# Joining MLP rounds in pairs: W1 with 512 moving columns, units ordered by row lane

## Chip, cores, metric

One core of one Trainium2 chip. The metric is the device time of one execution in microseconds (us), median over executions. A ratio is the mean time of one kernel's fast runs over the mean of the other's fast runs of the same rounds, so it is not quite the ratio of the medians quoted beside it.

## The reference

A transformer block on 2048 tokens of 576 features: layernorm, linear attention with a softmax feature map (32 heads of 18), output projection `wo`, residual; then layernorm and an MLP of 4608 hidden features. The part that matters here is the MLP:

```python
def _B_ref(x, w1, b1, w2, b2):          # x: 2048 x 576
    y = _layernorm(x, axis=-1)
    h = _gelu(jnp.einsum("bsd,df->bsf", y, w1) + b1)      # 576 -> 4608
    return jnp.einsum("bsf,fd->bsd", h, w2) + b2          # 4608 -> 576
...
h  = x + _A_ref(_layernorm(x), ...)     # attention and wo
h2 = h + _B_ref(_layernorm(h), ...)
```

## The kernel before

The MLP works in eight rounds of 256 tokens (two tiles of 128). A round is a W1 stage (36 blocks of 128 hidden features, gelu on ScalarE into `hmid`) and a W2 stage (two tiles, 36 matmuls of 512 columns and 36 of 64 each). The attention of later tiles is spread over it: `attn_N` (numerator and denominator, a chain on the vector engine and the pool engine behind it) in W2, `wo` with the second layernorm in W1.

W1 contracts over 576 = 4 x 128 + 64 rows. It runs in two row lanes, `pe0` (partitions 0 to 63) and `pe8` (64 to 127), that work side by side. Each unit is one PSUM bank with two blocks of 256 columns. Each lane does 4 half chunks per block, and the half chunk of 64 rows (`c == 4`) goes to one lane or the other. Both lanes add into the same bank, one after the other; which lane is first alternates.

```python
UNITS = [(4 * (u // 2) + u % 2, 4 * (u // 2) + u % 2 + 2) for u in range(NF // 2)]
...
def w1_half(r, u, h, begin):
    lane = "pe8" if h else "pe0"
    ...
    k = 1 if h else 0
    return [lambda i=i, c=c, n=n: one(i, c, begin and n == 0)
            for n, (i, c) in enumerate([(k, 4)] + [(i, c) for i in (0, 1) for c in range(4)])]

SKEW = 3
def w1_round(r, extra):
    lo, hi = [], []
    for s in range(NF // 2):
        k = s % 3
        u8 = s + (2, -1, -1)[k]             # second lane: units 2, 0, 1 of each three
        lo += [(f, None) for f in w1_half(r, s, 0, k < 2)]
        hi += [(f, None) for f in w1_half(r, u8, 64, k == 0)]
        # ... gelu of finished units, wo of later tiles
    hi = [(None, None)] * SKEW + hi         # first lane three matmuls ahead in issue order
    # ... then issued in turn, one of each lane

def w2_tile(r, j, slots):
    mb = (3, 2)[j]                          # PSUM bank of the 512 columns
    for i in range(NF + LAG):
        if i in slots:
            slots[i]()                      # attn_N of a later tile at step i
        # ... matmul i into bank mb, matmul i - LAG into the tail bank 4
    P.add("pool", ...tmpo = x_all[t] + b2bc...)
    # ... two vector additions ostage = psum + tmpo, then the output DMA
```

A scheduler class records every operation with the buffers and banks it touches and derives the semaphore waits. Each engine executes its stream in the order in which the operations are recorded.

The softmax here doesn't subtract the row's maximum and nothing guards it: scores larger than these inputs give would overflow.

## Time and profile before

| | before |
|---|---|
| median of 3 runs | 405.87 us (405.58 to 406.34) |
| span of the profiled run | 403.8 us |
| TensorE busy | 98% |
| W1 alone / W2 alone (256 tokens) | 18.02 / 17.75 us |
| from the first W1 to the last weight load of W2 | 309.48 us |

### The profile page before, as it was taken

The page shows a single profiled execution, that of the slowest core. Times are in us where ns is not written, and L with a number is a line of the kernel's source. Part 1 is how long each engine was busy: PE and PEld are TensorE (multiplying, and loading weights), DVE is VectorE, ACT ScalarE, POOL GpSimd, SP SyncE. Part 2 cuts the span into 40 slices and gives each one's busy share as a digit, 9 for nine tenths or more (in the row PEclk, how much of TensorE's full clock was granted, in tenths as well). Part 3 has the DMA queues.
Part 4 walks back from the last instruction along what each step waited for, and adds up shares of the span by engine and source line. Part 5 has one row for each costly group of instructions (what it writes and reads, how often), then busy time and mean ns, then how long its engine had stood idle before and what let it go on. Part 6 is the DMA issues. An engine that isn't in the chain of part 4 may idle for free.

```text
span 403.8 us, 11636 instructions
## 1 busy us (share of the span) xinstructions
PE 396.6 (98%) x4999; PEld 289.8 (72%) x4999; DVE 176.8 (44%) x415; ACT 184.4 (46%) x429; POOL 91.5 (23%) x130
## 2 busy tenths in 40 slices
PE   7999999999999999999999999999999999999997
PEld 4566666868955995599569856985797579658954
DVE  7999898876254223432442333243225312300000
ACT  6898955678820462057106600760175026404710
POOL 4759640112114002200220022002200220111001
PEclk9999999999999999999999999999999999999999
DMA  8586487981101101101111111001100110000000
GB/s 255 102 130 159 139 176 256 317 281 19 35 18 36 29 19 33 32 18 19 35 31 29 22 28 38 18 19 32 33 18 19 31 32 19 19 15 18 2 2 29
DMA packets 45738, 25.86 MB, mean 64 GB/s; under 512 B 32888, under 2 KB 44664, under 8 KB 45688
## 3 DMA queue, kind: packets, MB, share of 16 engines
q1 hardware_dynamic: 44928, 24.97, 24.8%
q8 instruction: 39, 0.64, 0.7%
q10 hardware_dynamic: 760, 0.17, 0.2%
q14 instruction: 11, 0.09, 0.1%
HBM read 15.13 MB, written 2.36 MB: 43 GB/s over the span
## 4 chain that ended last, share of the span: by engine, by line
PE 90%; DVE 5%; DMA 2%; ACT 1%; issue 1%; POOL 0%; DVEq 0%; ACTq 0%
PE ps_all L1153 35%; PE ps_all L1237 33%; PE ps_all L957 5%; PE ps_all L745 4%; PE ps_all L762 4%; PE ps_all L835 3%; PE ps_all L857 2%; PE ps_all L1220 2%; PE ps_all L804 2%; DMA yT<-ybuf 1%; DVE bns L494 1%; DMA x_all<-in_A_x_dram 1%; DVE sums L773 1%; DVE ybuf L526 1%; DVE x_all L979 1%
## 5 line engine op out<-in xcount | busy, mean ns | idle before, releaser
L1164 ACT ACTIVATE RA<-ps_all,b1T 128x256 bf16<-128x256 f32 x288 | 114.9, 478 | 176.8 <-PE ps_all L1153 162.1
L1153 PE MATMUL ps_all<-yT,w1sb 64*128 64x256 bf16 x2304 | 151.9, 269 | 0.0
L1153 PEld LDWEIGHTS ps_all<-yT,w1sb 64*128 64x128 bf16 x2304 | 136.1, 94 | 5.1
L1237 PE MATMUL ps_all<-w2a,RA 128*128 128x64 bf16 (+1 forms) x600 | 90.3, 286 | 0.0
L1153 PE MATMUL ps_all<-yT,w1t 64*128 64x256 bf16 x288 | 70.9, 270 | 0.0
L1237 PEld LDWEIGHTS ps_all<-w2a,RA 128*128 128x128 bf16 x600 | 42.9, 98 | 33.4 <-ACT RA L1164 1.7
L1237 PE MATMUL ps_all<-RB,RA 128*128 128x64 bf16 (+1 forms) x480 | 63.4, 286 | 0.0
L1246 DVE TENSOR_TENSOR WQ<-ps_all,tmpo 128x64 bf16<-128x64 f32 (+1 forms) x30 | 13.7, 458 | 96.3 <-PE ps_all L1237 84.0
L1237 PEld LDWEIGHTS ps_all<-RB,RA 128*128 128x128 bf16 x480 | 31.4, 98 | 30.3
L979 DVE SCALAR_TENSOR_TENSOR x_all<-ps_all,x_all 128x576 bf16<-128x576 f32 x16 | 12.1, 758 | 82.8 <-PE ps_all L957 82.8
L1001 POOL TENSOR_TENSOR st<-st,neghalf 128x1 f32<-128x1 f32 x16 | 8.8, 550 | 136.3 <-DVE st L998 133.6
L925 POOL TENSOR_TENSOR obuf<-tpn 128x576 bf16<-128x576 f32 x14 | 19.6, 1401 | 84.1 <-DVE tpn L918 74.4
L841 ACT ACTIVATE Eq<-ps_all 128x512 bf16<-128x512 f32 (+1 forms) x48 | 25.0, 526 | 12.2 <-PE ps_all L835 11.3
L957 PE MATMUL ps_all<-wo_sb,OTR 64*128 64x288 bf16 x288 | 29.7, 283 | 0.5 <-ACT OTR L567 0.2
L1153 PEld LDWEIGHTS ps_all<-yT,w1t 64*128 64x128 bf16 x288 | 26.3, 94 | 1.9
L835 PE MATMUL ps_all<-yT,WQ 128*128 128x256 bf16 x200 | 25.2, 273 | 0.2 <-ACT Eq L841 0.2
L786 DVE TENSOR_TENSOR RB<-ps_all,RB 128x1152 bf16<-128x1152 f32 x16 | 21.6, 1352 | 3.4 <-PE ps_all L762 3.3
L1243 POOL TENSOR_TENSOR tmpo<-x_all,b2bc 128x576 f32<-128x576 bf16 x15 | 19.1, 1272 | 17.4 <-DVE WQ L1246 17.4
L745 PE MATMUL ps_all<-RA,yT 128*128 128x512 bf16 (+1 forms) x160 | 22.4, 286 | 0.3 <-DMA yT<-ybuf 0.2
L957 PEld LDWEIGHTS ps_all<-wo_sb,OTR 64*128 64x128 bf16 x288 | 19.6, 94 | 3.7 <-PE ps_all L957 0.8
L762 PE MATMUL ps_all<-RB,yT 128*128 128x512 bf16 (+1 forms) x160 | 22.2, 286 | 0.0
L752 ACT ACTIVATE RB<-ps_all 128x576 bf16<-128x576 f32 x32 | 19.1, 649 | 5.8 <-PE ps_all L745 5.3
(110 smaller groups left out, 332.4 us busy)
## 6 DMA issues: line engine op xcount, KB each, us to landing
w1sb<-in_B_w_dram SPq DMA_DIRECT2D x8, 576.0 KB, 5.4
w2a<-in_B_w_dram SPq DMA_DIRECT2D x4, 720.0 KB, 7.3
RB<-in_B_w_dram SPq DMA_DIRECT2D x2, 1152.0 KB, 8.2
out_dram<-WQ SPq DMA_DIRECT2D x15, 144.0 KB, 1.8
x_all<-in_A_x_dram SPq DMA_DIRECT2D x3, 576.0 KB, 5.7
w2a<-in_A_wqkv_dram SPq DMA_DIRECT2D x2, 288.0 KB, 3.5
RB<-in_A_wqkv_dram SPq DMA_DIRECT2D x1, 576.0 KB, 5.7
w1t<-in_B_w_dram SPq DMA_DIRECT2D x2, 288.0 KB, 3.4
```

The source lines that it names most:

```text
L745: P.add("pe", lambda e, c=c, o=o, n=n: e.matmul(ps_all[:, 512 * KB + o:512 * KB + o + n], yT[:, c, sl * 128:(sl + 1) * 128], weffk[:, c, o ...
L752: P.add("act", lambda e, s=s: e.activation(Ek[eb][:, D * s:D * s + D], ps_all[:, 512 * KB:512 * KB + D], AF.Exp, scale=1.0 if s == 0 else ...
L762: P.add("pe", lambda e, c=c, o=o, n=n: e.matmul(ps_all[:, 512 * VB + o:512 * VB + o + n], yT[:, c, sl * 128:(sl + 1) * 128], wv[:, c, o:o ...
L786: P.add("dve", lambda e, s0=s0, s1=s1: e.tensor_tensor(vx(t)[:, s0:s1, :, 0:DH], ps_all[:, 512 * VB:512 * VB + D].rearrange("p (h d) -> p ...
L835: P.add("pe", lambda e, i=i, c=c, h0=h0: e.matmul(ps_all[:, 512 * bk + RW * i:512 * bk + RW * i + RW], weffq[:, c, DH * h0:DH * h0 + 128], ...
L841: P.add("act", lambda e, s=s: e.activation(Eq[:, r, s, bs[0]:bs[0] + n, :], ps_all[:, 512 * bk:512 * bk + RW * n].rearrange("p (b t) -> p ...
L925: P.add(oeng, lambda e: e.tensor_tensor(obuf[ob][:, 0:D], tpn[:, 0, :], tpn[:, 1, :], ALU.add), reads=[res("tpn")], writes=[res(f"obuf{ob}")])
L957: P.add(lane, lambda e: e.matmul(ps_all[:, 512 * bk:512 * bk + DHF], oT[ob][h:h + 64, c, :], wo_sb[h:h + 64, c, o:o + DHF], start=first, s ...
L1153: P.add(lane, lambda e: e.matmul(ps_all[:, o:o + RW], lhs, yT[h:h + 64, c, ys], start=first, stop=not begin and i == 1 and c == 3, skip_gr ...
L1164: P.add("act", lambda e, m=m, o=o: e.activation(hmid[:, m, :], ps_all[:, o:o + RW], AF.Gelu_apprx_tanh, bias=b1T[:, m:m + 1]), reads=[res( ...
L1237: P.add("pe", lambda e, m=m, bk=bk, o=o, n=n: e.matmul(ps_all[:, 512 * bk:512 * bk + n], w2_lhs(m, j), w2_rhs(m, o, n), start=(m == 0), st ...
L1243: P.add("pool", lambda e: e.tensor_tensor(tmpo[:, :], x_all[:, t, :], b2bc[:, :], ALU.add), reads=[res("b2"), res(f"x{t}")], writes=[res(" ...
```

## The change

The intent: from round three on, two rounds are joined to 512 tokens. A W1 unit is then one block of 512 columns, so half as many matmuls and weight loads are issued, and four W2 tiles follow one W1. The gelu output of 512 tokens is twice as large; half of it goes to the q features `Eq`, no longer needed by then. Blocks are ordered so that the second lane gets more work in the first units and the first lane in the last. With joined rounds, `attn_N` of four tiles must fit into W2 of round one and of round two, and `wo` of four tiles into W1 of round two, so their steps change, and the pool addition of each W2 tile is issued at its start (`BADD = 0`).

```diff
+    def mord(n):
+        lo, hi = [m for m in range(NF) if m % 4 < 2], [m for m in range(NF) if m % 4 >= 2]
+        if n == 1:
+            kinds = ["hh", "lh", "hh"] + ["lh"] * 12 + ["ll", "ll", "lh"]
+        else:
+            kinds = ["h"] * 3 + ["l", "h"] * 15 + ["l"] * 3
+        return [tuple((lo if k == "l" else hi).pop(0) for k in u) for u in kinds]
...
-        hi = [(None, None)] * SKEW + hi
-        # ... one of each lane in turn
+        at = [0, 0]
+        while lo or hi:
+            k = 0 if lo and (not hi or at[0] <= at[1] and hi[0][1]) else 1
+            f, w = (lo, hi)[k].pop(0)
+            f()
+            at[k] += w + (6 if w else 0)
...
+    BADD = 0
...
+            if i == BADD:
+                P.add("pool", ...tmpo = x_all[t] + b2bc...)
             if i in slots:
                 slots[i]()
...
-    for r in range(NR):
-        # ... attn_N of two tiles per W2 stage, steps 2 and 6; wo at units 3 and 12
+    GROUPS = [(0,), (1,), (2, 3), (4, 5), (6, 7)]
+    for g, rs in enumerate(GROUPS):
+        # ... wo of the next group; attn_N of the group after it:
+        j, i = (k // 2, ((4, 25) if g == 0 and k < 2 else (2, 22))[k % 2]) if len(here) == 2 else (k, 6)
```

## The prediction

> **What bounds the kernel now.** I read the page's busy shares first, then the chain that ended last in order of time, then a table of busy time by stage, then the groups by line and shape, and last the starts of single matmuls in the trace.
>
> The page:
>
> ```profile
> PE 396.6 (98%) x4999; PEld 289.8 (72%) x4999; DVE 176.8 (44%) x415; ACT 184.4 (46%) x429; POOL 91.5 (23%) x130
> ...
> PEclk9999999999999999999999999999999999999999
> ...
> PE 90%; DVE 5%; DMA 2%; ACT 1%; issue 1%; POOL 0%; DVEq 0%; ACTq 0%
> PE ps_all L1153 35%; PE ps_all L1237 33%; PE ps_all L957 5%; PE ps_all L745 4%; PE ps_all L762 4%; PE ps_all L835 3%; PE ps_all L857 2%; PE ps_all L1220 2%; PE ps_all L804 2%; DMA yT<-ybuf 1%; DVE bns L494 1%; DMA x_all<-in_A_x_dram 1%; DVE sums L773 1%; DVE ybuf L526 1%; DVE x_all L979 1%
> ```
>
> TensorE is the bound, at full clock, and two thirds of the chain is the MLP: W1 (L1153) and W2 (L1237). A busy share of 98% does not say that every slot is filled, so I go to the stages. The table by stage (columns: window, its length, TensorE busy with records, granted clock, DMA share, GB/s) gives, for rounds one and two, round seven and the W1 of round eight, a W1 row and a W2 row each:
>
> ```profile
> 91.63:112.73 21.10, 21.10 (x373) 1.00 0.17 26
> 112.73:131.96 19.23, 19.06 (x165) 1.00 0.16 34
> 131.96:152.19 20.23, 20.23 (x364) 1.00 0.07 18
> 152.19:171.09 18.90, 18.90 (x166) 1.00 0.17 35
> ...
> 327.58:347.80 20.22, 20.22 (x364) 1.00 0.07 17
> 347.80:365.55 17.75, 17.75 (x146) 1.00 0.08 20
> 365.55:383.57 18.02, 18.02 (x328) 1.00 0.03 10
> ```
>
> W1 alone takes 18.02 us (last row). With the two wo tiles of the next round it takes 20.22, so wo costs 2.20. W2 alone takes 17.75, and with two attn_N tiles 18.90. Round one's W2 is 0.33 longer than round two's, and its TensorE is short of its window by 0.17. The groups by line and shape:
>
> ```profile
> L1153 PE MATMUL ps_all<-yT,w1sb 64*128 64x256 bf16 x2304 | 151.9, 269 | 0.0
> L1153 PEld LDWEIGHTS ps_all<-yT,w1sb 64*128 64x128 bf16 x2304 | 136.1, 94 | 5.1
> L1164 ACT ACTIVATE RA<-ps_all,b1T 128x256 bf16<-128x256 f32 x288 | 114.9, 478 | 176.8 <-PE ps_all L1153 162.1 <-PE ps_all L957 13.6
> L1237 PE MATMUL ps_all<-w2a,RA 128*128 128x512 bf16 x300 | 75.2, 380 | 0.0
> L841 ACT ACTIVATE Eq<-ps_all 128x512 bf16<-128x512 f32 x32 | 19.1, 598 | 7.3 <-PE ps_all L835 6.8
> L841 ACT ACTIVATE Eq<-ps_all 128x256 bf16<-128x256 f32 x16 | 6.1, 383 | 4.9 <-PE ps_all L835 4.5
> ```
>
> W1 uses half the rows of the array per matmul (64*128), in two lanes that run side by side. The mean 269 ns is start to end; what counts is start to start. In the last W1 the trace shows pairs (one matmul of each lane) 109.3 ns apart. At the end the pairing stops: starts at 383.133 and 383.145, then single ones at 383.254 and 383.363. A round has 324 matmuls, 162 slots for two lanes: 162 x 0.1093 = 17.71. From 365.546 to the first W2 start at 383.565 are 18.02; less 0.093 of switch (202 ns between the last W1 start and the first of W2, less 109), 17.93 are left, or 164.1 slots. So two slots of each W1 are run by one lane alone.
>
> Why: a unit is a PSUM bank, which the lanes fill in turn, and the second waits for the first one's last matmul to complete. That is 269 ns plus some 60 of semaphore (DVE's end to the next weight load was 55 ns), or 3.0 slots after its start. Both lanes have nine matmuls per unit, so the second is due one slot after that start and is two late. The lag stays for the round.
>
> **What the Trainium skill says.** "TensorE: Matmul & The Clock Gate", section "Back-to-back issue gap", gives N/2.4 + 2.5 ns for the gap at full clock: 109.2 at 256 columns, 215.8 at 512. The trace agrees: 109.3 for the paired lanes, 215 to 217 for the 512-wide matmuls of W2. The same section's "sustained" 131 ns at 512 is not seen here. The page "TensorEngine Tiling (Array Packing)", section "Key Properties", says that changing the tiling mode drains the engine; the trace shows 93 ns over the usual gap going from W1 to W2 and 97 going back. "PSUM — Partial Sum Buffer", section "PSUM bank collisions raise a hardware error", says that two row tiles must not write one bank at the same time. That is why the lanes take turns and why the lag exists.
>
> **The change part by part.**
>
> Moving size 512. Three pairs of rounds have 3 x 324 matmuls of 512 in place of 6 x 324 of 256. Per pair, 2 x 162 x 109.2 = 35.38 become 162 x 215.8 = 34.96: 0.42 saved. The weight loads halve, but they lay beside the matmuls (94 against 109 ns), so this is worth nothing by itself.
>
> Order by row lane. The half chunk of 64 rows belongs to one lane or the other by block. Three blocks whose half chunk is the second lane's come first, three of the other kind last. In a pair the second lane so has 5 slots in its first unit while the first has 4: it is due at slot 5, and the first lane's bank is complete at 3 + (380 + 60)/216 = 5.04. Later handoffs have more room, and both lanes end together at 162. This saves 2.1 slots of 0.109 per joined round: 0.23, or 0.46 per pair. In rounds one and two (units of two blocks) the first handoff fits too (10 against 10.02), but the last one does not: the second lane is due in its last unit at slot 154, and the bank is complete at 155.02. One slot stays lost, so 0.12 is saved per round.
>
> Mode switches. Four W2 tiles follow each joined W1: one W1-to-W2 and one W2-to-W1 switch less per pair, 0.19.
>
> Gelu. In W1, 256 columns follow one another every 356 ns (six in 2.29 us). For 512 I estimate 478 + (598 - 383) = 693 ns, against 4.5 x 216 = 971 per unit on TensorE: hidden, and ScalarE gets more room than before (712 of 983). But the last pair unit in bank 3 is finished by the second lane only 5 slots before W1 ends, and W2's first tile starts in bank 3. The completion is 1.08 - 0.38 = 0.70 before that end, gelu starts 0.22 later (382.65 to 382.87 in the trace) and ends at +0.21, and with 0.06 of semaphore W2 starts at +0.27 in place of +0.09. New wait: 0.17 per pair.
>
> Sum per pair: 0.42 + 0.46 + 0.19 - 0.17 = 0.90; three pairs 2.70. Rounds one and two: 0.24.
>
> attn_N moved. The count of attn_N and wo matmuls stays the same. The first attn_N in round one's W2 is moved from step 2 to step 4, after the wait seen here:
>
> ```profile
> 113.72 0.34 PEld L857 LDWEIGHTS ps_all<-kvr,Eq 126*128 126x128 bf16 x6 [0.33 <-DVE x_all L979]
> ```
>
> That 0.33 goes. But now two attn_N fall into each W2 tile of rounds one and two. The vector chain of one (L872 at 153.28 to the end of L918 at 156.80) is 3.52 us. In round one it starts behind the LayerNorm chain of the last wo, which I put at 116.5, so it ends at 120.0. The second attn_N wants the banks from 119.55: about 0.1 of wait, and at the next tile 0.16 more. I take the gain as 0.33 - 0.26 = 0.07. In round two there is room.
>
> The pool addition moved to the start of a W2 tile, the output buffers and the added oT buffers move nothing on TensorE. The output addition at a W1 start frees bank 2 in time: done 0.83 after that start, wanted at 0.86 (4 slots of 216).
>
> Total: 2.70 + 0.24 + 0.07 = 3.0. 405.87 - 3.0 = 402.9. The step positions look tuned to avoid just these waits, so I go slightly lower: 402.6.
>
> **The rivals.**
>
> 1. New waits eat the gain. Several margins are tens of ns: 5.04 against 5, 0.86 against 0.83, the bank 3 wait at 0.17. For it: the operands wait in program order, so one lane's wait also stops the other. Against it: each is a wait once per round, not per unit. If each pair lost two 512 slots again (0.43 x 3), the time would be 403.9.
> 2. ScalarE becomes the bound in W1. If gelu were to take over 971 ns at 512 columns, the pairs would run at its pace, each 0.01 us longer per unit for every 10 ns: at 1100 ns some 4.6 us more per pair, a slower kernel. Exp at 512 took 598 against 383, so I give this almost nothing.
> 3. 512-wide lanes gain more than the gap formula says, if weight loads now disturb the 256-wide stream. Then W1 would fall clearly below 34.96 per pair. Against it: pairs at 109.3 ns leave 2.6 over 256/2.4, so at most 0.0026 x 972 = 2.5 us could be had in all, of which 1.26 is counted. That bounds the time near 400.9.
> 4. The joining crowds DVE and Pool with attn_N and output work: those engines are at 44% and 23%, and this would show only in rounds one and two. Worth at most 1 us.
>
> **Range and chances.** Rivals 1 and 4 give the upper side, 403.9; skipping all new waits (0.51 for bank 3, 0.26 for attn_N) gives 402.1, and some of rival 3 a bit less. I take 401.5 to 403.9. Faster by over 2% needs 397.8, 8.1 us, more than twice what can be found. Slower by 2% needs rival 2. Chances: 0.02 faster, 0.97 the same, 0.01 slower.
>
> **What would show it.** Pair slots of 215 to 217 ns; W1 of the last pair, which has no wo in it, at 35.0 to 35.3 us and both lanes ending within one slot; four W2 tiles at 35.5 without attn_N; a TensorE idle of 0.1 to 0.3 on ScalarE at each W1-to-W2 border; the first W1 at 20.98. It is wrong if slots differ from 216, if single-lane stretches remain in the pairs, or if DVE waits appear on TensorE in the W2 of the first two rounds that sum to over 0.5 us.

## More of the kernel before

The prediction shows the lines that carry its argument. Two more matter later. They are from the timelines of the vector engine and of pool in round one's W2 (columns: start in us, duration in us, engine, line, operation, output and inputs, and what ended the idle time before):

```profile
115.65 0.43 DVE L526 TENSOR_SCALAR ybuf<-x_all,st 128x576 bf16<-128x576 bf16 x1 [0.74 <-POOL st L1001]
```

```profile
121.48 1.27 POOL L1243 TENSOR_TENSOR tmpo<-x_all,b2bc 128x576 f32<-128x576 bf16 x1
```

The first is the layernorm of the last `wo` tile, which runs at the start of W2. The second is the pool addition for the output of the first W2 tile. It comes almost 6 us later, when the normalisation is long done.

## The result

| | before | after |
|---|---|---|
| median, same rounds | 406.07 us | 404.04 us (403.80 to 404.56) |
| ratio, 95% interval | | 0.9953 (0.9936 to 0.9970) |
| span of the profiled run | 403.8 us | 402.1 us |
| first W1 to last weight load of W2 | 309.48 us | 307.35 us |

The kernel is faster by 2.0 us. The prediction, 402.6 with 401.5 to 403.9, wanted 3.3 and missed its range by 0.14. The class (within 2%) was right. Two later calls ran the changed kernel again: 404.36 and 404.05, ratios 0.9946 both times.

A caution on reading: the trace of the changed kernel has 4,027 weight loads but 3,990 matmuls; 37 matmul records are missing, among them the first of several stages. By matmul records the border from W1 to W2 seemed to have grown by 0.2 to 0.3 us everywhere. The weight loads are complete, and I take all stage borders at them.

The page of the changed kernel:

```profile
PE 390.9 (97%) x3990; PEld 240.9 (60%) x4027; DVE 182.6 (45%) x415; ACT 169.3 (42%) x321; POOL 92.0 (23%) x130
...
PEclk9999999999999999999999999999999999999999
```

TensorE is still the bound. Its table by stage, counted at weight loads (columns: window, length, busy time of weight loads with their number, clock, DMA share, GB/s; the edges are rounded to 0.01, so a row here or below can differ by 0.01 from the lengths that I quote):

```profile
91.48:112.27 20.79, 18.45 (x371) 1.00 0.15 27
112.27:133.75 21.48, 11.38 (x185) 1.00 0.18 38
133.75:156.28 22.53, 20.07 (x396) 1.00 0.35 38
156.28:176.33 20.05, 11.45 (x184) 1.00 0.25 42
176.33:215.89 39.56, 22.59 (x397) 1.00 0.11 22
215.89:253.58 37.69, 20.52 (x330) 1.00 0.14 34
...
328.50:363.65 35.15, 17.25 (x325) 1.00 0.02 5
```

The rows are W1 and W2 of round one, of round two, and of the first pair; the last is the W1 of the last pair, which has neither `wo` nor `attn_N` in it: 35.15 for 512 tokens, where two old rounds took 2 x 18.02. Round one's W2 (second row) is the odd one: round two's W2 (fourth row) does the same work, four `attn_N` and two tiles, in 1.43 less.

The groups by line and shape show the new sizes:

```profile
L1182 PE MATMUL ps_all<-yT,w1sb 64*128 64x512 bf16 x864 | 113.4, 376 | 0.0
L1200 ACT ACTIVATE Eq<-ps_all,b1T 128x512 bf16<-128x512 f32 x54 | 35.3, 685 | 18.7 <-PE ps_all L1182 18.0
```

The gelu takes 685 ns (estimate 693), so it is hidden. The waits of the weight loads (columns: total us, times, longest) and the timeline at the start of round one's W2:

```profile
PEld ps_all L869 <- DVE tpn L926: 1.9, 2, 1.1
PEld ps_all L1266 <- ACT Eq L1200: 1.4, 3, 0.5
...
PEld ps_all L1182 <- DVE WQ L1272: 1.0, 4, 0.3
```

```profile
115.08 1.28 POOL L1260 TENSOR_TENSOR tmpo<-x_all,b2bc 128x576 f32<-128x576 bf16 x1
115.22 1.30 DVE L538 TENSOR_SCALAR ybuf<-x_all,st 128x576 bf16<-128x576 bf16 x1 [0.74 <-POOL st L1014]
```

The first wait is new in kind: `attn_N` matmuls (L869) wait for the vector multiplication of the `attn_N` before (L926), twice, both in round one's W2. This view counts all the time between two weight loads. What is lost I take from the starts of the matmuls: 0.952 us from the one before where about 0.03 is usual behind a matmul of 64 columns, and 0.702 where 0.216 is usual behind one of 512, so 0.92 and 0.49. The timeline shows a reason for the first. The pool addition, now at the start of the tile, begins just before the layernorm of the last `wo` tile, which takes 1.30 us where it took 0.43, and ends 0.16 after the addition.

Where the time went, stage by stage, with the moved work taken out (two `attn_N` are 1.15: 18.898 - 17.747; two `wo` are 2.20: 20.223 - 18.019):

| stage | before | after | work moved in or out | change | predicted |
|---|---|---|---|---|---|
| W1 of round one | 21.10 | 20.79 | 0 | -0.31 | -0.12 |
| W2 of round one | 19.24 | 21.48 | +1.15 | +1.10 | -0.07 |
| W1 of round two | 20.22 | 22.53 | +2.20 | +0.11 | -0.12 |
| W2 of round two | 18.90 | 20.05 | +1.15 | 0.00 | 0 |
| rounds three and four | 78.24 | 77.25 | 0 | -1.00 | -0.90 |
| rounds five and six | 78.24 | 74.92 | -2.30 | -1.02 | -0.90 |
| rounds seven and eight | 73.53 | 70.33 | -2.20 | -1.00 | -0.90 |
| sum | | | 0 | -2.13 | -3.0 |

The joined rounds gave what was predicted and a little more. Round one's W2 took 1.17 more than its step allowed: 0.92 + 0.49 came where 0.1 + 0.16 was forecast.

Stage lengths repeat within 0.02 us from profile to profile. What lies outside does not: the first W1 started anywhere from 91.5 to 94.2, and from the last weight load to the end took 2.74 to 3.95, in kernels with the same code there. I therefore judge by stages first and by medians second.

### The profile page after: what moved, and what is told of

Read it like the earlier page. It is cut to its first block, busy times and chain, and to the rows that moved or that the text cites. A ratio compares the mean times of both kernels' runs of the same rounds, so it can differ in the third digit from the quotient of the medians.

```text
span 402.1 us, 9487 instructions
## 1 busy us (share of the span) xinstructions
PE 390.9 (97%) x3990; PEld 240.9 (60%) x4027; DVE 182.6 (45%) x415; ACT 169.3 (42%) x321; POOL 92.0 (23%) x130
## 4 chain that ended last, share of the span: by engine, by line
PE 68%; DVE 2%; issue 1%; DVEq 0%
PE ps_all L1182 31%; PE ps_all L1266 30%; PE ps_all L970 3%; PE ps_all L1244 2%; PE ps_all L869 2%; DVE tpn L926 1%; DVE ds L898 0%; DVE den L914 0%; DVE ds L884 0%; DVE pr L906 0%; DVE aa L915 0%; DVE ds L888 0%; DVE den L908 0%; DVE WQ L1248 0%; DVE ybuf L541 0%
## 5 line engine op out<-in xcount | busy, mean ns | idle before, releaser
L1182 PE MATMUL ps_all<-yT,w1sb 64*128 64x512 bf16 (+1 forms) x1440 | 154.3, 333 | 0.0
L1200 ACT ACTIVATE RA<-ps_all,b1T 128x256 bf16<-128x256 f32 (+1 forms) x126 | 65.7, 566 | 153.2 <-PE ps_all L1182 150.3
L1182 PEld LDWEIGHTS ps_all<-yT,w1sb 64*128 64x128 bf16 x1440 | 87.0, 94 | 43.5 <-DVE WQ L1272 0.7
L1272 DVE TENSOR_TENSOR WQ<-ps_all,tmpo 128x64 bf16<-128x64 f32 (+1 forms) x30 | 13.7, 458 | 110.0 <-PE ps_all L1266 109.3
L1182 PE MATMUL ps_all<-yT,w1t 64*128 64x512 bf16 (+1 forms) x180 | 58.7, 334 | 0.0
L1266 PE MATMUL ps_all<-RB,Eq 128*128 128x512 bf16 (+1 forms) x344 | 45.8, 284 | 0.3
L1200 ACT ACTIVATE Eq<-ps_all,b1T 128x512 bf16<-128x512 f32 x54 | 35.3, 685 | 18.7 <-PE ps_all L1182 18.0
L1266 PEld LDWEIGHTS ps_all<-RB,Eq 128*128 128x128 bf16 x352 | 23.0, 98 | 22.3
L774 PE MATMUL ps_all<-RB,yT 128*128 128x64 bf16 (+1 forms) x157 | 21.7, 284 | 0.2
L757 PE MATMUL ps_all<-RA,yT 128*128 128x64 bf16 (+1 forms) x152 | 20.6, 281 | 0.8 <-ACT RA L614 0.2
L785 DVE TENSOR_REDUCE sums<-RB 128x64 f32<-128x1152 bf16 x16 | 21.4, 1338 | 0.0
```

The costliest lines, as they stand in the source:

```text
L757: P.add("pe", lambda e, c=c, o=o, n=n: e.matmul(ps_all[:, 512 * KB + o:512 * KB + o + n], yT[:, c, sl * 128:(sl + 1) * 128], weffk[:, c, o ...
L774: P.add("pe", lambda e, c=c, o=o, n=n: e.matmul(ps_all[:, 512 * VB + o:512 * VB + o + n], yT[:, c, sl * 128:(sl + 1) * 128], wv[:, c, o:o ...
L785: P.add("dve", lambda e: e.tensor_reduce(sums[vb][:, :], Ek[eb][:, 0:1152].rearrange("p (h f) -> p h f", h=64), AX.X, ALU.add), reads=[res ...
L1182: P.add(lane, lambda e: e.matmul(ps_all[:, o:o + w], lhs, yT[h:h + 64, c, ys], start=first, stop=last, skip_group_check=True), reads=rd + ...
L1200: P.add("act", lambda e, m=m, o=o: e.activation(hm(n, m), ps_all[:, o:o + RW * n], AF.Gelu_apprx_tanh, bias=b1T[:, m:m + 1]), reads=[res(" ...
L1266: P.add("pe", lambda e, m=m, bk=bk, o=o, w=w: e.matmul(ps_all[:, 512 * bk:512 * bk + w], w2_lhs(n, m, j), w2_rhs(m, o, w), start=(m == 0), ...
```

## The experiments

Theory A: the pool addition at the start of the tile stretches the vector chain. Theory L: a lane waits for the other one's last matmul in each bank, and the order of blocks only hides or shows this. (A slot is the time in which each lane does one matmul: 109 ns at 256 columns, 216 at 512.) The rivals are named with each run.

### e1 and e11: the changed kernel again

No edit.

> The changed kernel once more, unedited, as the yardstick of this call and to see which of its stage lengths repeat. Both theories: 404.0 within 0.4. Theory A (waits of round one are fixed by the order of instructions): the W2 of round one takes 21.48 within 0.05 again, with a TensorE wait of some 0.9 and one of 0.5 on the vector engine. Theory T (the end is longer because an instruction fetch falls into the last output transfers, as the trace of the first run shows 1.0 us before the end of TensorE): from the last vector addition to the end 2.9 us again, against 2.4 in the kernel before. Rival of T: chance; then it is 2.4 here.

> The changed kernel unedited as the yardstick of this call: 404.1 within 0.4; from the first W1 to the last TensorE instruction 307.37 within 0.03; W2 of round one 21.48 within 0.05.

Measured: 404.36 and 404.05; W2 of round one 21.49 and 21.48; from first W1 to last weight load 307.37 and 307.35. Theory T, that a late instruction fetch lengthens the end, was not tested by these two runs, for neither has such a fetch before its end: from the last weight load to the end they took 2.79 us, about as long as the kernel before (2.74). The other traces speak for it. The seven profiles without a fetch there take 2.74 to 2.79 us. In the first run of the changed kernel, e6 and e8 a fetch of 16 KB ran until 1.09, 1.25 and 0.80 us after the last weight load; the issue of the last output transfer, which starts at 0.68, then took 0.78, 0.95 and 0.50 in place of 0.33, and the end was longer by just that (3.24, 3.40, 2.96). In e2 the fetch lay among the transfers themselves (3.95). In e5 and e7 it was over by 0.59 and 0.71, and the end was 2.79. No run moved a fetch on purpose, and why it comes when it does stays open.

### e2: the first pool addition early

```diff
-            if i == BADD:
+            if i == BADD and t > 0:
...
+            extra[6] = [((), (), lambda: P.add("pool", ...tmpo = x_all[0] + b2bc...))]   # in W1 of round one
```

> The changed kernel with one edit: the pool addition for the first W2 tile is issued in the W1 of round one, where pool and the vector engine are idle, so that it no longer runs beside the LayerNorm of the last wo tile. Theory A (the pool addition at the start of the tile makes the vector normalisation wait: 1.30 us in place of 0.43, and the attn_N chain behind it and TensorE with it): the normalisation takes 0.43 again, the 0.92 us wait of TensorE falls to 0.1 or less, the W2 of round one takes 20.5 to 20.7 in place of 21.48, the whole kernel gets 0.8 to 1.0 faster. Rival B (two attn_N per W2 tile are too many for the vector engine, whatever pool does): the wait falls by 0.2 at most, and the time stays within 0.2.

Measured: 403.30 (402.58 to 404.65), ratio 0.9924. The timeline of the vector engine, three operations of round one's W2, that of pool, and the stage:

```profile
116.22 0.43 DVE L538 TENSOR_SCALAR ybuf<-x_all,st 128x576 bf16<-128x576 bf16 x1 [0.73 <-POOL st L1014]
...
117.37 0.19 DVE L898 SCALAR_TENSOR_TENSOR ds<-ds 128x32 f32<-128x32 f32 x1
...
121.15 0.71 DVE L898 SCALAR_TENSOR_TENSOR ds<-ds 128x32 f32<-128x32 f32 x1
```

```profile
120.41 1.40 POOL L937 TENSOR_TENSOR obuf<-tpn 128x576 bf16<-128x576 f32 x1 [4.30 <-issue]
```

```profile
113.26:133.88 20.62, 11.38 (x185) 1.00 0.19 40
```

The normalisation is back at 0.43. The first wait of TensorE fell from 0.92 to 0.05, and the stage from 21.48 to 20.61. Theory A holds, and rival B falls for this wait. It agrees with the Trainium skill, "SBUF — State Buffer", section "Who interferes with whom": the vector engine in a two-port mode and GpSimd share one pair of ports, and the one that issues second blocks for the whole instruction. (That the normalisation runs in such a mode is not shown here; its times fit.) The second wait, 0.49, is untouched. Its chain has an operation with two SBUF inputs (L898) that takes 0.71 in place of 0.19 while pool adds up `obuf`; the same section says that such operations contend too. No run took the `obuf` addition alone away, so this second cause is read from the traces and not tested.

### e3 and e5: the old order in joined rounds

```diff
-            kinds = ["hh", "lh", "hh"] + ["lh"] * 12 + ["ll", "ll", "lh"]
+            kinds = ["lh"] * 18
...
-            kinds = ["h"] * 3 + ["l", "h"] * 15 + ["l"] * 3
+            kinds = ["l", "h"] * 18
...
-        at = [0, 0]
+        at = [0, 3 * (RW * n + 6)]     # e5 only: the old head start in issue order
```

> The changed kernel with the old order of blocks (kinds alternate, none put first), joined rounds kept. Theory L (the second lane waits for the first one's last matmul to complete in each bank, so an order without a head start leaves it two slots late, 0.44 us at 512 columns and 0.22 at 256, to the end of the round): the last joined W1 takes 35.5 to 35.6 in place of 35.15, with two matmuls of one lane alone at its end, and the kernel is 1.5 to 1.9 slower than the changed one. Rival M (the order does nothing, the joining alone brought the gain): 35.15 and no change in time.

e3 measured 436.66 us and a wrong result (relative error 0.055); the last W1 took 45.09. Both expectations missed. I had taken the order alone for the remedy and forgotten that the old order came with a head start of three matmuls in the order of issue. Without it both lanes stop together, three times in six units: the last W1 has 18 gaps of 0.435 to 1.03 us between starts where 0.216 is usual. The shortest, six of 0.435 or 0.436, are the 0.376 of a 512-wide matmul and 0.06: by the order of issue, the second lane's wait for the first lane's bank stands just ahead of the first lane's next matmul. Six longer ones wait for a gelu, and the code says why: in every sixth unit the gelu is recorded before the first lane's last matmul of that bank, which also explains the wrong result. Neither happens in e5 (no gap there over 0.216), nor in the new order (0.223 at most), which is therefore also what makes the streams without head start correct.

> Joined rounds with the old order of blocks, and the old head start of three slots for the first lane in the order of issue (left out in e3, where an activation could be issued ahead of the first lane's last matmul). The result should be right again. Theory L: the lag of two slots is back, so the last joined W1 takes 35.5 to 35.65 in place of 35.15, with two or three matmuls of one lane alone at its end, the other joined W1 0.4 to 0.5 more each, and the kernel is 1.2 to 1.9 us slower than the changed one: 405.5 to 406.2 where that is 404.2. Rival M: 35.15, no change.

e5 is correct: 406.54, ratio 1.0021. The last W1:

```profile
330.89:366.68 35.79, 19.00 (x324) 1.00 0.02 5
```

It takes 0.64 more than 35.15, more than I expected. At its end one lane runs alone for two matmuls (starts at 365.900 and 366.116), 0.43 us, and W2 then waits 0.2 more for a gelu. Rival M falls. From first W1 to last weight load e5 takes 309.75, more than the kernel before (309.48): joining with the old order and these steps gains nothing, since the 1.0 that the pairs win is lost in rounds one and two.

### e4: the order alone

All rounds single, old steps for `attn_N` and `wo`, pool addition at the end of the tile, new order:

```diff
-    GROUPS = [(0,), (1,), (2, 3), (4, 5), (6, 7)]
+    GROUPS = [(r,) for r in range(NR)]
...
-    BADD = 0
+    BADD = NF + LAG - 1
```

> All rounds single as in the kernel before (256 columns, attn_N at the old steps, pool addition at the end of the tile), but the new order of blocks. Theory L: each W1 loses its two single-lane slots but keeps one at its end, so the last W1 takes 17.8 to 17.9 in place of 18.02, rounds two to seven 0.1 to 0.3 less each, and the kernel is 1.0 to 2.4 us faster than the kernel before, that is 403.7 to 405.1. Rival M: as before, 406.0.

Measured: 405.12, ratio 0.9967. The last W1:

```profile
365.15:383.06 17.91, 16.85 (x324) 1.00 0.03 10
```

That is 18.02 less one slot of 0.109, as theory L has it: of two single-lane slots one stays. From first W1 to last weight load 308.44: the order alone is worth 1.05. That is no share of the 2.13, for the gains do not add: the joining alone costs 0.26 (e5), and in joined rounds the order is worth 2.39 (309.75 less 307.35).

### e6 and e7: moving attn_N in round one's second tile

Both on top of e2. In e6 the steps (2, 22) of the second tile become (5, 24), and the joined W2 begins in bank 2 (the last tile, handled apart, moves from bank 2 to 3):

```diff
-        mb = (3, 2)[j % 2]
+        mb = (3, 2)[j % 2] if n == 1 else (2, 3)[j % 2]
```

In e7, with the same banks as e6, the steps are (5, 23), and the pool addition of the second tile comes after its first `attn_N`:

```diff
-            if i == BADD and t > 0:
+            if i == (6 if t == 1 else BADD) and t > 0:
...
-        j, i = ... (4, 25) if g == 0 and k < 2 else (2, 22) ...
+        j, i = ... (4, 25) if g == 0 and k < 2 else (5, 23) if g == 0 else (2, 22) ...   # e6: (5, 24)
```

> The early pool addition of e2, and two edits in other stages: in the second W2 tile of round one the attn_N go from steps 2 and 22 to 5 and 24 (theory C: the remaining wait of 0.49 is only the vector chain of the attn_N before, which the pool addition for obuf stretched; three steps of 0.245 more cover it, W2 of round one 20.1 to 20.3 in place of 20.61); and in the joined rounds the first W2 tile writes bank 2 in place of bank 3 (theory G: of the 369 ns between the last W1 start and the first W2 load, some 60 to 170 are the wait for the gelu of the last unit in bank 3; the last W1 then takes 34.98 to 35.09 in place of 35.15; rival: the 369 are drain of a 512-wide matmul, and 35.15 stays). Time: 0.5 to 0.9 us less than e2, that is 402.4 to 402.8 where e2 is 403.3.

> As e6, but with steps 5 and 23 and the pool addition of the second W2 tile issued after its first attn_N. Theory A again (pool additions beside the small vector operations stretch the chain: one took 1.17 in place of 0.19 us in e2): the chain of the third attn_N gets 0.9 shorter, TensorE needs not wait at step 23, and the vector addition at the end of the tile is not late, so the W1 of round two takes 22.3 to 22.4 in place of 22.53. Rival: the addition now stretches the chain of the fourth attn_N, and W1 of round two stays at 22.5 or gets longer.

e6 measured 403.72, ratio 0.9950, where 402.4 to 402.8 was expected. Its W2 of round one, W1 of round two and last W1:

```profile
113.26:133.38 20.12, 11.42 (x186) 1.00 0.17 36
133.38:156.41 23.03, 20.07 (x397) 1.00 0.37 42
328.52:363.60 35.08, 17.24 (x324) 1.00 0.02 5
```

Theory C holds for the stage: 20.11 in place of 20.61. But the 0.50 was given back at once, for W1 of round two grew from 22.53 to 23.03. The vector chain of the fourth `attn_N` ends as late as in e2 (21.05 after the start of W2 in both), so the output addition behind it is late, and W1 waits for the bank that it empties. e7 (403.49, ratio 0.9943) shows it more strongly: W2 20.11, W1 of round two 23.28. The later pool addition stretched an operation of the fourth chain to 1.23 us (0.23 without). Its forecast for that W1 (22.3 to 22.4) missed, and its rival was right.

The last W1 answers the other question: exchanging the bank takes 0.065 off it (35.148 to 35.083). So the gelu wait at the border was 0.065, not 0.17. Another 0.107 of what I saw at the border is just what a 512-wide matmul takes more than a 256-wide one (376 against 269 ns to its end, 216 against 109 to the next start).

### e8: the pool addition at the end, as before

```diff
-    BADD = 0
+    BADD = NF + LAG - 1
```

> The changed kernel with the pool addition of each W2 tile issued at the tile's end as in the kernel before. Theory A with its other side: no 0.92 wait at the first attn_N pair of round one, but with two attn_N in a tile pool comes to the addition only after both obuf additions, so the output additions of the tiles of rounds one and two are late by 2 to 3 us each and TensorE waits for the tail bank at step 5 of the next tile: W2 of round one 22 to 25 in place of 21.48, W2 of round two 21 to 24 in place of 20.05; the joined rounds unchanged. The kernel 2 to 6 us slower than the changed one. Rival: pool has room enough, W2 of round one 20.6, all else the same, 403.3.

Measured: 418.16, ratio 1.0282. Pool and vector timelines of round one's W2:

```profile
125.99 1.27 POOL L1260 TENSOR_TENSOR tmpo<-x_all,b2bc 128x576 f32<-128x576 bf16 x1
```

```profile
127.39 0.95 DVE L1272 TENSOR_TENSOR WQ<-ps_all,tmpo 128x64 bf16<-128x64 f32 x2 [3.17 <-POOL tmpo L1260]
```

The vector engine idles 3.17 us for the addition. It did so in the kernel before too; but there the addition stood behind one `obuf` addition and began 8.76 us after the start of W2, here it stands behind two and begins at 13.14. The W2 of round one takes 24.69, of round two 21.67, as expected in kind; the W1 after them suffer too (26.96 in place of 22.53, and 44.35 in place of 39.56), which I had not expected, and the granted clock fell to 0.93 and 0.94 in two of these stages. The kernel lost 14 us where I had expected 2 to 6. Its weight loads wait 11.8 us for the output additions (1.0 in the changed kernel); how much of the rest is the clock is not separated. So the change needed the early addition; only its place beside the layernorm was unlucky.

### e9: the banks alone

W1 of round two exchanges banks 2 and 3, and the W2 tiles from round two on begin in bank 2 (the last tile, handled apart, moves from bank 2 to 3). No other edit.

```diff
+    def ubank(rs, u):
+        return {2: 3, 3: 2}.get(UBANK[u], UBANK[u]) if rs == (1,) else UBANK[u]
...
-        mb = (3, 2)[j % 2]
+        mb = (3, 2)[j % 2] if t < RT else (2, 3)[j % 2]
```

> The changed kernel with one edit: the banks of the W2 tiles and of the W1 of round two are exchanged so that no W1 begins in a bank that the W2 tile before it has just filled (in rounds one and two and in the joined rounds). Theory D (the 0.2 us that W1 of round two loses 1.1 us after its start is the wait for a vector addition that comes late behind the attn_N chain): W1 of round two 22.31 to 22.35 in place of 22.53; the last W1 35.08 as in e6; the W2 of round one stays at 21.48, since its waits have another cause. Kernel 0.3 to 0.5 us faster than the changed one. Rival: the wait is for the tail bank 4, which stays: 22.53.

Measured: 403.83, ratio 0.9943. W2 of round one and W1 of round two:

```profile
114.97:136.46 21.49, 11.36 (x186) 1.00 0.18 38
136.46:158.78 22.32, 21.08 (x397) 1.00 0.32 39
```

Theory D holds: the 0.21 were the wait for a late output addition in the bank with which W1 begins. The waits inside W2 stay, as expected.

### e10: all together

e2, the steps (5, 24), e9's banks, and one more edit for rounds one and two:

```diff
-            kinds = ["hh", "lh", "hh"] + ["lh"] * 12 + ["ll", "ll", "lh"]
+            kinds = ["hh", "lh", "hh"] + ["lh"] * 12 + ["lh", "ll", "ll"]
```

> All edits that helped together: early pool addition, steps 5 and 24, exchanged banks, and in rounds one and two the three last units in an order that leaves the second lane room (theory L: the one slot of 0.109 us that one lane still runs alone is gone). Expected: W1 of round one 20.68, W2 of round one 20.11, W1 of round two 22.2 to 22.25 (e6 had 23.03 because the vector addition came late; with exchanged banks this costs nothing), pairs as in e6. From the first W1 to the last TensorE instruction 305.4 to 305.6, 1.8 us less than the changed kernel, 3.9 less than the kernel before: 402.0 to 402.4 where that is 406. Rival: the late additions move the wait to bank 4 and W1 of round two stays over 22.5.

Measured: 402.31 (401.74 to 402.71), ratio 0.9903 (0.9889 to 0.9916), where the changed kernel had 0.9946. W1 and W2 of round one, W1 of round two, last W1:

```profile
92.37:113.16 20.79, 18.53 (x371) 1.00 0.15 27
113.16:133.27 20.11, 11.42 (x185) 1.00 0.16 36
133.27:155.48 22.21, 21.14 (x396) 1.00 0.34 43
327.59:362.68 35.09, 17.36 (x325) 1.00 0.02 5
```

From first W1 to last weight load 305.49, as expected (305.4 to 305.6). With the banks exchanged, the time won in W2 is no longer given back. The new order of the last units takes exactly one slot off W1 of round two (22.32 to 22.21). In W1 of round one it does nothing; there the expectation of 20.68 missed.

## Why the prediction was wrong

**What failed.** The step "attn_N moved", with the sentence that "the pool addition moved to the start of a W2 tile, the output buffers and the added oT buffers move nothing on TensorE". I had put the two waits of round one at 0.1 and 0.16; they were 0.92 and 0.49. The first forecast is 0.82 too small because of the pool addition: it delays the layernorm, the layernorm delays the first `attn_N` chain, and the second `attn_N` waits for that chain's banks. e2 shows this by taking only the addition away: 0.92 becomes 0.05. The second is 0.33 too small, by the traces because pool's `obuf` addition runs beside the next chain (0.19 to 0.71 for one operation); this was not tested alone. I had timed that chain where nothing overlapped it, at 3.52; here it takes 4.08. I had looked at the busy shares of pool and vector engine (rival 4, "at most 1 us"), and these say nothing about two instructions that meet. The prediction had named this sign of being wrong, DVE waits in the W2 of the first two rounds of over 0.5 us in sum: they were 1.41.

**A smaller miss of the same kind.** "The output addition at a W1 start frees bank 2 in time" was true for the joined rounds but not for round two, where a chain stands in front of the addition: 0.21, shown by e9. That is nearly all of the 0.23 by which W1 of round two came out worse than its step.

**What held.** Slots of 215.8 to 216 ns, W1 of the last pair at 35.15 (predicted 35.0 to 35.3), gelu hidden, TensorE the bound. The lag of two slots and the remaining one in single rounds (e4: 0.109 to the third digit). Per pair 1.00 came in place of 0.90, since the gelu wait was 0.065 and not 0.17 (e6).

**What else was off.** W1 of round one gained 0.31 in place of 0.12. The order does it (e4 has 20.79 too, e5 with the old order 21.10), but why there is no single-lane slot left at its end is open; it is the only W1 with an `attn_N` in it. The traces show where the 0.31 lies. In the kernel before, one matmul stands alone just ahead of that `attn_N`, which starts 4.364 us into W1, and three `wo` matmuls of one lane stand alone at the end of the stage. In the changed kernel none does: `attn_N` starts at 4.268, and the rest of the stage is 0.22 shorter. That this W1 alone ends with `wo`, in other banks, is a second candidate for the reason; neither was tested. And the last adjustment, from 402.9 to 402.6 because "the step positions look tuned", went the wrong way: the waits were there, and e10 with other steps and banks takes 1.86 less between first W1 and last weight load. Without it the miss would have been 1.1 and not 1.4.

**Adding up.** Predicted by steps 3.0; less 1.17 (W2 of round one), less 0.23 (W1 of round two), plus 0.19 (W1 of round one), plus 0.3 (pairs) is 2.1, the 2.13 of the stages. The medians say 2.0 to 2.2. The two better terms were not foreseen; that they hid 0.49 of the 1.40 that the two worse ones cost was luck.

## What to carry to other kernels

When an instruction moves in time, ask what it will run beside, not only whether its engine has room: a pool addition of 1.3 us on an engine at 23% stopped a vector instruction, and through a chain of buffers TensorE. When a wait is shortened, look in the next stage for it: e6 won 0.50 and lost 0.50, and only a free bank there made the gain stay. And where two lanes share banks by turns, the order of issue is part of the design: the same matmuls without a head start cost 30 us (e3 against e5) and a wrong result.

## What the Trainium skill lacked or had wrong

- "TensorE: Matmul & The Clock Gate", "Back-to-back issue gap": the sustained 131 ns per matmul at 512 columns is not seen; paired lanes and full-array matmuls both run at 215 to 216. The formula N/2.4 + 2.5 holds for two row lanes side by side (109.3 and 215.8).
- The same page, "The mechanism" of Part 3, says that matmuls start in program order. In the kernel before, the second lane's first matmul is the fifth in order of issue and starts 13 ns after the first one. So here a lane ran ahead of the other once issued.
- No page has the cost of a handover between row lanes in one PSUM bank as a whole: completion of the last matmul (269 ns at 256 columns, 376 at 512; lengths of that kind the pages do have) plus some 60 (e3: 436 from start to start), so that the other lane is two slots late. An issue order without head start made that 10 to 12 us per joined W1 (e3: 45.09 against 35.15 in the last).
- "TensorEngine Tiling (Array Packing)" says that a mode switch drains the engine, without a figure: 93 to 97 ns over the usual gap with 256-wide matmuls.
- Nothing was wrong in "SBUF — State Buffer", "Who interferes with whom": it would have told me to look, 0.43 to 1.30 us for the blocked normalisation.
